# First key and query halves in banks of their own, longer transfer times in the planned order, and the last output tiles in score tile and free banks

## The chip, the cores and the metric

The kernel runs on one core of a Trainium2 chip. The metric is device time in microseconds (us) of one execution; three executions of the kernel before the change were timed. A profile of one more execution gives a span (from the first to the last instruction) and a record of every instruction and transfer. Engines are named as the profile names them: PE (TensorE matmuls), DVE (VectorE), ACT (ScalarE), POOL (GpSimd) and SP, the queue from which nearly all transfers (DMAs) are issued.

## The reference

A layer normalisation of x feeds two branches, whose outputs are added to x: causal attention with a memory that is carried over four segments of 512 tokens (32 heads of width 16), and a two-layer block with silu.

```python
x = A_x                                   # (1, 2048, 512), bf16
xn = _layernorm(x, axis=-1)
return x + _A_ref(xn, A_wq, A_wk, A_wv, A_wo, A_beta) + _B_ref(xn, B_w1, B_w2)

# _A_ref, for each segment s of 4, with q, k, v = xn @ wq, xn @ wk, xn @ wv by heads:
p = _softmax(qs @ ks.T * scale + mask)    # causal
a_dot = p @ vs
a_mem = (phi(qs) @ M) / (phi(qs) @ z + 1e-06)
o = g * a_mem + (1.0 - g) * a_dot         # g = sigmoid(beta)
M = M + phi(ks).T @ vs;  z = z + phi(ks).sum()
# after the segments: o @ wo

# _B_ref: silu(xn @ w1) @ w2, w1 (512, 1792), w2 (1792, 512)
```

## The kernel before

The program is written as a list of tasks. Each task has an engine, a duration `dur`, a time `vis` after which its result counts as visible to others, a due time, the tasks it depends on, and the buffers that it takes from a ring and gives back. `Sched.run` plays these tasks through with the durations and `vis` numbers written in the code, picks at each free engine the ready task with the earliest due time (with some rules of its own for scores, exponentials and evictions), and emits the instructions in the order in which they started in that play. That order is what each engine's instruction stream gets; an engine takes its stream in order, and an instruction whose input isn't there holds everything behind it on its engine. So a `vis` number that is too short puts a reader of a transfer too early in its engine's stream. `T0` and `CYC` set the due times (`Dn(n)`).

The on-chip accumulator memory is held as `psS`, one tile of four banks for the attention scores, and a ring `banks` of four single-bank tiles `ps66` to `ps69` for everything else. A write of PE into a bank tile waits until earlier reads of that tile are done, and a reader waits for the earlier writes.

The work of a segment s:

- `ln(s)`: statistics and normalised x (`xn`), transposed into `xnT` (segment 0 by PE and a copy, the others by transposing DMAs on SP).
- `k_tile`, `q_tile`, `v_tile`: `xnT` by `w_k`, `w_q`, `w_v`. Index u = 4 s + dt counts tiles of 128 of the 512 columns. `kB` is the key tile masked for even and odd heads, `kT` and `qT` the plain copies. The tile u = 0 goes through `first_tile`, in four pieces of 128 tokens, so that the first score can start early. `v_swap` makes `VS`, a copy of `V` with its partition halves swapped, by two DMAs.
- `quad(u, q)`: score n (`S{n}`) into `psS`, one exponential over 128x2048 on ACT (`E{n}`, tile `Pt`), and the causal mask on POOL (line 826). There are 72 of these. `pv` multiplies `Pt` by `V` and `VS`; DVE copies the results to `N` and `O`.
- `norm(s, dts)`: the softmax denominators of `N` and `O` go to DRAM (`dZ`), come back as `Zg`, are inverted by DVE (`Zf`, line 1028) and scaled by POOL (`Zr`), go to DRAM again (`dR`) and come back spread over all partitions as `R`; meanwhile `O` is merged into `N` by four DMAs. DVE multiplies `N` by `R` (line 1055). `den(s)` does the same for the memory's denominators (`dD`, `Dg`, `Dq`, `dE`, `Dr`), POOL multiplies `pq` by `Dr` (line 991), PE multiplies `pq` by the memory `Mbf`, and DVE adds that to `N` (line 1070). In the last segment `norm` runs for the first three column tiles, and then for the fourth alone.
- `h_tile`: xn by w1, tanh on ACT, gate on DVE (`hT`, line 1089). `w2_rows` and `wo_rows` give the output rows of segments 0 to 2.
- `tail()`: the last segment's four output tiles. Output tile j is 14 matmuls by `w_2` and 4 by `w_o`, all into `psS[:, j, :]`, then one eviction with the addition of x (`o_t`, line 1178) and a store.

Of the kernel before, what the change touches and what calls it, by code (L numbers as in the profile page):

```python
# [14 lines left out]
P = 128  # L15
# [6 lines left out]
NSEG = 4  # L22
# [19 lines left out]
NWARM = 44  # L42
# [4 lines left out]
PVW = 0.0  # L47

# [212 lines left out]
def kernel(  # L261
# [158 lines left out]
    load_x(12, 4, "SP", 0.7, 19.5)  # L420
# [117 lines left out]
    def ln(s, due):  # L538
        for half in range(2):
            ag = []  # L540
            for j in (2 * half, 2 * half + 1):
                t = s * TPS + j
                b = Buf(st_r)

                def f_st(t=t, b=b):
                    nc.vector.bn_stats(out=b.tile[:], in_=xt(t))
                    nc.vector.bn_aggr(out=mv[:, t, :], in_=b.tile[:])

                ag.append(A("DVE", 0.75, f_st, [xl[t]], due, takes=(b,), frees=(b,), label="stats"))
# [9 lines left out]
            for j in (2 * half, 2 * half + 1):  # L559
# [36 lines left out]
                else:  # L596
# [5 lines left out]
                    e = A("SP", 1.25, f_d, [n], due, vis=2.7, takes=(xnT_b[s],),  # L602
# [34 lines left out]
    def first_tile(w, loads, due, label):  # L637
        b = Buf(banks)
        pcs = []
        for j in range(TPS):  # L640
            c = slice(j * P, (j + 1) * P)

            def f(c=c):
                for ki in range(DT):
                    mm(b.tile[:, c], w[:, ki, 0:P], xnT_b[0].tile[:, ki, c], ki == 0, ki == DT - 1)
            pcs.append(A("PE", 0.26, f, [xnT_done[0][j], loads], due + 0.01 * j, takes=(b,),
                         frees=(b, xnT_b[0]), mode="full", label=label))
        return b, pcs
# [4 lines left out]
    def k_tile(s, dt, due):  # L653
        u = 4 * s + dt
        kT[u], kB[u] = Buf(kT_r), Buf(kB_r)
        if u == 0:
            b, pcs = first_tile(w_k, ld_k[0], due, "k0")
            kb_ev[u] = []
            for hf in range(2):
                c = slice(256 * hf, 256 * hf + 256)  # L660
                for r in range(2):
                    def f_e(c=c, r=r, hf=hf):
                        o = half(kB[u].tile, r, hf)
                        i = b.tile[:, c].rearrange("p (a b) -> p a b", b=KB)
                        if r == 0:
                            nc.scalar.mul(o, i, pm[:, 0:1])
                        else:
                            nc.vector.tensor_scalar(
                                out=o, in0=i, scalar1=pm[:, 1:2], scalar2=None, op0=ALU.mult
                            )  # L670
                    kb_ev[u].append(A(
                        "DVE" if r else "ACT", 0.3, f_e, pcs[2 * hf : 2 * hf + 2] + [c_pm], due + 0.5,
                        takes=(kB[u],), frees=(b, kB[u]), label="k0"))
            ev = A("DVE", 0.6, lambda: nc.vector.tensor_copy(out=kT[u].tile[:], in_=b.tile[:]),
                   pcs, due + 3, takes=(kT[u],), frees=(b, kT[u]), label="kT")
        else:
# [5 lines left out]
            ev = A("DVE", 0.6, lambda: nc.vector.tensor_copy(out=kT[u].tile[:], in_=b.tile[:]),  # L682
                   [g], due + 1.5, takes=(kT[u],), frees=(b, kT[u]), label="kT")
            kb_ev[u] = []
            for r in range(2):
                def f_o(r=r):
                    nc.gpsimd.tensor_scalar(  # L687
                        out=kB[u].tile[:, :, KB * r : KB * r + KB],
                        in0=kT[u].tile[:].rearrange("p (a b) -> p a b", b=KB),
                        scalar1=pm[:, r : r + 1], scalar2=1.0, op0=ALU.mult, op1=ALU.mult,  # L690
                    )
                kb_ev[u].append(pool(0.75, f_o, [ev, c_pm], due + 3, takes=(kB[u],),
                                     frees=(kT[u], kB[u]), label="kB"))
        if s < NSEG - 1:
            pb = Buf(pkT_r)
            zc = zc_t[s % 2][:, dt : dt + 1]
            f = phi(kT[u], pb, [ev], Dn(5 * u + 7), zc)
# [6 lines left out]
            e = A("SP", 1.25, f_t, [f], Dn(5 * u + 9), vis=2.7,  # L704
# [3 lines left out]
    def q_tile(s, dt, due):  # L708
        u = 4 * s + dt
        qT[u] = Buf(qT_r)  # L710
        if u == 0:
            b, pcs = first_tile(w_q, ld_q[0], due, "q0")
            q_ev[u] = []
            for hf in range(2):
                c = slice(256 * hf, 256 * hf + 256)

                def f_e(c=c, hf=hf):
                    if hf:
                        nc.scalar.copy(out=qT[u].tile[:, c], in_=b.tile[:, c])
                    else:  # L720
                        nc.vector.tensor_copy(out=qT[u].tile[:, c], in_=b.tile[:, c])
                q_ev[u].append(A("ACT" if hf else "DVE", 0.3, f_e, pcs[2 * hf : 2 * hf + 2],
                                 due + 0.5, takes=(qT[u],), frees=(b, qT[u]), label="q0"))
# [30 lines left out]
    def v_swap(s, due):  # L754
        ts = []
        for r in range(2):
# [3 lines left out]
            ts.append(A("SP", 0.5, f, v_ev[s], due, vis=3.5, takes=(VS_b[s],),  # L760
# [26 lines left out]
    def quad(u, q):  # L787
# [16 lines left out]
        deps = [d for uu in us for d in kb_ev[uu] + q_ev[uu]]  # L804
# [127 lines left out]
    def den(s, due):  # L932
# [25 lines left out]
        d1 = A("SP", 0.58, f_1, [e], due + 2, vis=2.7, frees=(db,), label="den")  # L958
# [3 lines left out]
        d2 = A("SP", 0.4, f_2, [d1], due + 3, vis=2.0, label="den")  # L962
# [14 lines left out]
        d3 = A("SP", 0.35, f_5, [r2], due + 6, vis=1.6, label="den")  # L977
        for dt in range(DT):
# [9 lines left out]
            d4 = A("SP", 0.45, f_6, [d3], due + 7, vis=3.6, takes=(rb,), frees=(rb,), label="den")  # L988
# [9 lines left out]
    def norm(s, dts, due, due_rep):  # L998
# [6 lines left out]
        for par in range(2):  # L1005
# [7 lines left out]
            zs.append(A("SP", 0.55, f_1, ev, due, vis=2.0, frees=(N_b[s] if par == 0 else O_b[s],),  # L1013
# [4 lines left out]
        d2 = A("SP", 0.45, f_2, zs, due + 1, vis=1.95, label="Z")  # L1018
        mg = []
        for g in range(4):  # L1020
# [3 lines left out]
            mg.append(A("SP", 0.6, f_m, [zs[0]] + [O_ev[4 * s + d] for d in dts] + [E_ev[4 * s + d] for d in dts], due + 1.5, vis=2.6,  # L1024
# [16 lines left out]
        d3 = A("SP", 0.35, f_5, [r2], due + 1, vis=1.6, label="Z")  # L1041
        for dt in dts:
# [8 lines left out]
            d4 = A("SP", 0.45, f_6, [d3], due + 1, vis=3.6, takes=(rb,), frees=(rb,), label="Z")  # L1051
# [96 lines left out]
    def tail():  # L1148
        s = NSEG - 1
        for j in range(TPS):  # L1150
            b = Fixed(psS[:, j, :])
            t = s * TPS + j

            def s2(ft, b=b, j=j):
                def f():
                    mm(b.tile[:], h_b[(s, ft)].tile[:, j * P : (j + 1) * P], w_2[:, ft, :],
                       ft == 0, False)
                return (f, 0.216, (h_ev[(s, ft)],))

# [14 lines left out]
            o.frees.append(N_b[s])  # L1174
            ob = Buf(o_r)

            def f_e(b=b, ob=ob, t=t):
                nc.vector.scalar_tensor_tensor(  # L1178
                    out=ob.tile[:], in0=b.tile[:], scalar=0.5, in1=xt(t), op0=ALU.mult,
                    op1=ALU.add,  # L1180
                )
            e = A("DVE", 0.6, f_e, [o], -2, takes=(ob,), frees=(ob,), label="o_t")
# [6 lines left out]
    for s in range(NSEG):  # L1189
# [3 lines left out]
        if s == 0:  # L1193
            for dt in range(DT):
                k_tile(0, dt, -2.9 if dt == 0 else Dn(5 * dt - 3 - dt % 2))
                q_tile(0, dt, -3 if dt == 0 else Dn(5 * dt - 2.9 - dt % 2))
                if dt == 0:
                    for j in range(TPS):
                        v_tile(0, j, Dn(0.2 + 0.7 * j))
                    v_swap(0, Dn(2))  # L1200
# [63 lines left out]
```

## Time and profile before

| what | value |
|---|---|
| three timed executions | 254.0, 255.46, 252.55 us; median 254.0 |
| profiled execution | own time 251.29 us, span 249.6 us |
| PE busy | 225.4 us, 90% of the span |
| DVE, ACT, POOL busy | 170.4, 178.4, 165.3 us |
| mean granted PE clock | 0.992 |
| transfers | 21.33 MB, 85 GB/s on average, up to 359 GB/s in the first 25 us |

The busy share of an engine is an average over stages. Where an engine stands idle, the profile names in square brackets what ended the wait and how long it was. The profiled execution's own time is 1.7 us longer than its span.

### The profile page before, as it was taken

The page shows a single profiled execution, that of the slowest core. Times are in us where ns is not written, and L with a number is a line of the kernel's source. Part 1 is how long each engine was busy: PE and PEld are TensorE (multiplying, and loading weights), DVE is VectorE, ACT ScalarE, POOL GpSimd, SP SyncE. Part 2 cuts the span into 40 slices and gives each one's busy share as a digit, 9 for nine tenths or more (in the row PEclk, how much of TensorE's full clock was granted, in tenths as well). Part 3 has the DMA queues.
Part 4 walks back from the last instruction along what each step waited for, and adds up shares of the span by engine and source line. Part 5 has one row for each costly group of instructions (what it writes and reads, how often), then busy time and mean ns, then how long its engine had stood idle before and what let it go on. Part 6 is the DMA issues. An engine that isn't in the chain of part 4 may idle for free.

```text
span 249.6 us, 6833 instructions
## 1 busy us (share of the span) xinstructions
PE 225.4 (90%) x2824; PEld 105.1 (42%) x2824; DVE 170.4 (68%) x298; ACT 178.4 (72%) x160; POOL 165.3 (66%) x279
## 2 busy tenths in 40 slices
PE   7889989989799869999898999999899999995973
PEld 7644344435343424443443444444353434441331
DVE  3569989977767647799824897766574866666132
ACT  2378978999788668978986898889968877720000
POOL 6328998789899488958865799479777455740000
PEclk9999999999999999999999999999999999999799
DMA  6999920014344242010364500133402000341001
GB/s 195 354 359 295 153 46 3 0 43 66 66 98 94 89 110 104 22 45 1 66 137 76 123 5 8 42 106 84 99 23 72 4 11 22 104 153 33 25 21 63
DMA packets 31068, 21.33 MB, mean 85 GB/s; under 512 B 16116, under 2 KB 30140, under 8 KB 31036
## 3 DMA queue, kind: packets, MB, share of 16 engines
q1 hardware_dynamic: 29692, 20.10, 31.4%
q10 hardware_dynamic: 1344, 0.79, 1.0%
q8 instruction: 22, 0.36, 0.6%
q14 instruction: 10, 0.08, 0.1%
HBM read 11.87 MB, written 2.65 MB: 58 GB/s over the span
## 4 chain that ended last, share of the span: by engine, by line
PE 40%; ACT 13%; DVE 13%; DMA 13%; POOL 10%; SPq 5%; issue 4%; ACTq 0%; DVEq 0%; POOLq 0%
PE ps L496 30%; ACT Pt L810 10%; PE psS L496 10%; POOL Pt L826 5%; DMA R<-dR 3%; DVE hT L1089 2%; DMA VS<-V 2%; DVE pkT L628 2%; DVE pq L628 2%; ACT hT L1085 2%; DMA dR<-Zr 2%; POOL kB L687 2%; DMA dZ<-O 1%; SPq L1047 1%; SPq L1023 1%
## 5 line engine op out<-in xcount | busy, mean ns | idle before, releaser
L810 ACT ACTIVATE Pt<-psS 128x2048 bf16<-128x2048 f32 x72 | 135.4, 1880 | 26.9 <-PE psS L496 24.0
L826 POOL TENSOR_SCALAR_AFFINE_SELECT Pt<-Pt 64x512 bf16<-64x512 bf16 (+1 forms) x144 | 94.3, 655 | 29.0 <-ACT Pt L810 23.9
L496 PE MATMUL ps<-xnT,w 128*128 128x512 bf16 x224 | 57.6, 380 | 0.0
L1089 DVE SCALAR_TENSOR_TENSOR hT<-hT,ps 128x512 bf16<-128x512 bf16 x56 | 37.2, 679 | 11.2 <-ACT hT L1085 11.2
L496 PE MATMUL ps<-w,hT 128*128 128x512 bf16 x168 | 41.9, 380 | 1.1 <-DVE acc L1114 1.1
L1085 ACT ACTIVATE hT<-ps 128x512 bf16<-128x512 f32 x56 | 32.1, 599 | 5.0 <-PE ps L496 5.0
L496 PEld LDWEIGHTS <-hT 128*128 128x128 bf16 x224 | 20.6, 99 | 31.3 <-issue 9.9
L496 PE MATMUL psS<-qT,kB 32*128 32x256 bf16 (+5 forms) x640 | 28.7, 261 | 2.9 <-ACT Pt L810 2.5
L496 PEld LDWEIGHTS <-w 128*128 128x128 bf16 x224 | 20.2, 98 | 24.5 <-issue 2.7
L687 POOL TENSOR_SCALAR kB<-kT,pm 128x512 bf16<-128x512 bf16 x30 | 21.6, 727 | 7.2 <-DVE kT L682 5.9
L496 PEld LDWEIGHTS <-kB 32*128 32x128 bf16 x640 | 12.5, 92 | 28.3 <-issue 27.1
L496 PE MATMUL ps<-Pt,VS 64*32 64x256 bf16 (+5 forms) x640 | 18.9, 261 | 3.4 <-DMA VS<-V 1.4
L496 PE MATMUL ps<-Pt,V 64*32 64x256 bf16 (+5 forms) x640 | 20.6, 260 | 0.2 <-DVE hT L1089 0.2
L496 PE MATMUL ps<-xnT,w_k 128*128 128x512 bf16 (+1 forms) x76 | 17.7, 346 | 2.6 <-DVE M L901 1.3
L496 PE MATMUL psS<-w,hT 128*128 128x512 bf16 x56 | 15.5, 401 | 3.1 <-DVE o_t L1178 2.3
L496 PE MATMUL ps<-xnT,w_q 128*128 128x512 bf16 (+1 forms) x76 | 17.2, 346 | 1.1 <-DVE hT L1089 0.8
L496 PE MATMUL ps<-w_v,xnT 128*128 128x512 bf16 x64 | 17.2, 380 | 0.0
L496 PEld LDWEIGHTS <-V 64*32 64x32 bf16 x640 | 13.7, 91 | 8.1 <-issue 3.2
L1055 DVE TENSOR_TENSOR N<-N,R 128x512 bf16<-128x512 bf16 x16 | 8.1, 510 | 12.0 <-DMA R<-dR 12.0
L869 DVE CAST N<-ps 128x512 bf16<-128x512 f32 x16 | 11.0, 687 | 7.7 <-PE ps L496 7.5
L496 PE MATMUL ps<-w_o,N 128*128 128x512 bf16 x48 | 12.9, 380 | 2.4 <-DVE N L1055 2.3
L496 PEld LDWEIGHTS <-VS 64*32 64x32 bf16 x640 | 12.7, 91 | 5.2 <-issue 1.8
(81 smaller groups left out, 261.8 us busy)
## 6 DMA issues: line engine op xcount, KB each, us to landing
VS<-V SPq DMA_DIRECT2D x8, 264.0 KB
R<-dR SPq DMA_DIRECT2D x16, 128.0 KB
out_dram<-o_t SPq DMA_DIRECT2D x16, 128.0 KB
w<-in_B_w_dram SPq DMA_DIRECT2D x2, 896.0 KB
w<-in_B_w_dram SPq DMA_DIRECT2D x1, 1792.0 KB
Dr<-dE SPq DMA_DIRECT2D x12, 128.0 KB
x_all<-in_A_x_dram SPq DMA_DIRECT2D x2, 512.0 KB
N<-O SPq DMA_DIRECT2D x12, 64.0 KB
```

The lines of the kernel that those rows point to most:

```text
L496: nc.tensor.matmul(o, lhsT=l, rhs=r, start=start, stop=stop, **k)
L628: nc.vector.scalar_tensor_tensor(out=dst_b.tile[:], in0=src_b.tile[:], scalar=0.0, in1=dst_b.tile[:], op0=ALU.max, op1=ALU.add, accum_out=acc,
L687: nc.gpsimd.tensor_scalar(out=kB[u].tile[:, :, KB * r : KB * r + KB], in0=kT[u].tile[:].rearrange("p (a b) -> p a b", b=KB), scalar1=pm[:, ...
L810: nc.scalar.activation(out=pb.tile[:], in_=psS[:], func=AF.Exp, scale=SCALE)
L826: nc.gpsimd.affine_select(out=v, in_=v, compare_op=ALU.is_ge, fill=0.0, base=0, pattern=pat, channel_multiplier=-1,)
L869: nc.vector.tensor_copy(out=dst.tile[:, dt, :], in_=buf.tile[:])
L1023: nc.sync.dma_start(out=N_b[s].tile[r, ds, :], in_=O_b[s].tile[r, ds, :])
L1047: nc.sync.dma_start(out=rb.tile[:], in_=dap(dR[i], (dt - dts[0]) * L, [[nd * L, 8], [0, DH], [1, L]]),)
L1055: nc.vector.tensor_tensor(out=v, in0=v, in1=rb.tile[:], op=ALU.mult)
L1085: nc.scalar.activation(out=hb.tile[:], in_=b.tile[:], func=AF.Tanh, scale=0.5)
L1089: nc.vector.scalar_tensor_tensor(out=hb.tile[:], in0=hb.tile[:], scalar=1.0, in1=b.tile[:], op0=ALU.add, op1=ALU.mult)
```

## The change

1. `first_tile` makes two of the four pieces of tile u = 0 per call, and `k_tile` and `q_tile` call it once for each half, so each half of the first key and query tile takes a bank tile of its own. `kT` of that tile is copied in two halves. Score 0 depends on the first half's `kB` pieces alone (and on both halves of `qT`). Six of the 44 pairs of filler matmuls (`NWARM`) go.
2. The `vis` numbers of nearly all transfers get longer: `dZ` 2.0 to 3.2 (2.5 for the last `norm`), `Zg` 1.95 to 2.6 (2.5), `R` 3.6 to 4.0 (3.2), `dD` 2.7 to 3.0, `Dg` 2.0 to 2.4, `Dr` 3.6 to 4.2, `xnT` 2.7 to 3.6, `VS` 3.5 to 6.0 in segment 0 and 4.2 in the others; the due times of V and `VS` in segment 0 move earlier. Since the order comes from these numbers, nearly every engine's stream changes in places.
3. In `tail()` output tiles 0 and 1 stay in `psS`, tiles 2 and 3 take bank tiles of the ring. The evictions of tiles 0 and 1 wait for both tiles; all evictions are written after all matmuls.

```diff
-NWARM = 44
+NWARM = 38
+ZW = (3.2, 2.5)
+ZG = (2.6, 2.5)
+ZD = (2.0, 1.6)
+ZR = (4.0, 3.2)
...
-    def first_tile(w, loads, due, label):
+    def first_tile(w, loads, due, label, hf):
         b = Buf(banks)
         pcs = []
-        for j in range(TPS):
-            c = slice(j * P, (j + 1) * P)
+        for j in (2 * hf, 2 * hf + 1):
+            c, o = slice(j * P, (j + 1) * P), slice((j % 2) * P, (j % 2) * P + P)
...
-            b, pcs = first_tile(w_k, ld_k[0], due, "k0")
-            kb_ev[u] = []
+            kb_ev[u], ev = [], []
             for hf in range(2):
-                c = slice(256 * hf, 256 * hf + 256)
+                b, pcs = first_tile(w_k, ld_k[0], due + 0.3 * hf, "k0", hf)
...
+                def f_c(hf=hf, b=b):
+                    nc.vector.tensor_copy(
+                        out=kT[u].tile[:, 256 * hf : 256 * hf + 256], in_=b.tile[:, 0:256]
+                    )
...
-            ts.append(A("SP", 0.5, f, v_ev[s], due, vis=3.5, takes=(VS_b[s],),
+            ts.append(A("SP", 0.6, f, v_ev[s], due, vis=6.0 if s == 0 else 4.2, takes=(VS_b[s],),
...
-        deps = [d for uu in us for d in kb_ev[uu] + q_ev[uu]]
+        deps = [d for uu in us for d in (kb_ev[uu][0:2] if n == 0 else kb_ev[uu]) + q_ev[uu]]
...
-        d2 = A("SP", 0.45, f_2, zs, due + 1, vis=1.95, label="Z")
+        d2 = A("SP", 0.55, f_2, zs, due + 1, vis=ZG[i == NSEG], label="Z")
...
-            b = Fixed(psS[:, j, :])
+            b = Fixed(psS[:, j, :]) if j < 2 else Buf(banks)
...
-            e = A("DVE", 0.6, f_e, [o], -2, takes=(ob,), frees=(ob,), label="o_t")
+            e = A("DVE", 0.6, f_e, [o] if j >= 2 else [ends[0][1], ends[1][1]], -2,
+                  takes=(ob,), frees=(ob,) + ((b,) if j >= 2 else ()), label="o_t")
...
-                        v_tile(0, j, Dn(0.2 + 0.7 * j))
-                    v_swap(0, Dn(2))
+                        v_tile(0, j, Dn(0.2 * j - 1))
+                    v_swap(0, Dn(-5))
```

Three places show how the streams move. The first is ACT at the program's start, from the copies that make `xnT` to the first exponential, `Pt_107<-psS`. Before:

```order
L590 COPY xnT_77<-ps_66 128x4x128
L590 COPY xnT_77<-ps_67 128x4x128
L590 COPY xnT_77<-ps_68 128x4x128
L719 CAST qT_90<-ps_66 128x256
L666 ACTIVATE kB_85<-ps_67,pm 128x4x64 x2
L619 ACTIVATE pkT_98<-kT_82 128x512
L810 ACTIVATE Pt_107<-psS 128x2048
```

and of the change:

```order
L594 COPY xnT_77<-ps_66 128x4x128
L594 COPY xnT_77<-ps_67 128x4x128
L594 COPY xnT_77<-ps_66 128x4x128
L669 ACTIVATE kB_85<-ps_69,pm 128x4x64
L727 CAST qT_90<-ps_68 128x256
L669 ACTIVATE kB_85<-ps_66,pm 128x4x64
L818 ACTIVATE Pt_107<-psS 128x2048
L623 ACTIVATE pkT_98<-kT_82 128x512
```

The two halves of `kB` now come from two banks, and the exponential of the memory's key tile (`pkT`) moves behind the first attention exponential.

The second is SP in the first segment's `norm` and the second segment's `den`, where `R` has three buffers, so that the fourth `R` (the second `R_139`) waits for the first to be used. Before:

```order
L1040 DMA dR_192<-Zr_176 128x128
L961 DMA Dg_179<-dD_198 128x128
L1047 DMA R_139<-dR_192 128x1x512
L1047 DMA R_140<-dR_192 128x1x512
L1047 DMA R_141<-dR_192 128x1x512
L976 DMA dE_202<-Dq_181 128x128
L984 DMA Dr_142<-dE_202 128x1x512
L984 DMA Dr_143<-dE_202 128x1x512
L1047 DMA R_139<-dR_192 128x1x512
```

and of the change:

```order
L1048 DMA dR_192<-Zr_176 128x128
L709 DMA_TRANSPOSE phiK_100<-pkT_99 128x4x128
L1055 DMA R_139<-dR_192 128x1x512
L1055 DMA R_140<-dR_192 128x1x512
L1055 DMA R_141<-dR_192 128x1x512
L969 DMA Dg_179<-dD_198 128x128
L1055 DMA R_139<-dR_192 128x1x512
L984 DMA dE_202<-Dq_181 128x128
```

The fourth `R` now stands ahead of `dE` and of both `Dr`, and `Dg` behind the first three `R`.

The third is SP in the last segment, from the first `norm`'s way back (`dR_195`) to the last `norm`'s read (`Zg_172`). Before:

```order
L1040 DMA dR_195<-Zr_177 96x128
L1145 DMA out_dram<-o_t_150 128x512
L1047 DMA R_139<-dR_195 128x1x512
L1047 DMA R_140<-dR_195 128x1x512
L1047 DMA R_141<-dR_195 128x1x512
L1145 DMA out_dram<-o_t_151 128x512
L1008 DMA dZ_191<-N_137 4x512
L1008 DMA dZ_191<-O_138 4x512
L1023 DMA N_137<-O_138 16x512
L1017 DMA Zg_172<-dZ_191 32x128
```

and of the change:

```order
L1048 DMA dR_195<-Zr_177 96x128
L1153 DMA out_dram<-o_t_150 128x512
L1055 DMA R_139<-dR_195 128x1x512
L1016 DMA dZ_191<-N_137 4x512
L1016 DMA dZ_191<-O_138 4x512
L1055 DMA R_140<-dR_195 128x1x512
L1055 DMA R_141<-dR_195 128x1x512
L1153 DMA out_dram<-o_t_151 128x512
L1031 DMA N_137<-O_138 16x512
L1025 DMA Zg_172<-dZ_191 32x128
```

The two `dZ` writes pass two `R` reads and a store. On POOL at the same time, the last causal mask, `Pt_108`, moved ahead of the multiplications of `pq` by `Dr`. Before:

```order
L826 AFFINE_SELECT Pt_107<-Pt_107 64x8x64 x2
L991 TENSOR_TENSOR pq_103<-pq_103,Dr_144 128x512
L1033 TENSOR_SCALAR Zr_177<-Zf_175,gcol 96x128
L991 TENSOR_TENSOR pq_104<-pq_104,Dr_142 128x512
L826 AFFINE_SELECT Pt_108<-Pt_108 64x8x64 x2
```

and of the change:

```order
L834 AFFINE_SELECT Pt_107<-Pt_107 64x8x64 x2
L834 AFFINE_SELECT Pt_108<-Pt_108 64x8x64 x2
L1041 TENSOR_SCALAR Zr_177<-Zf_175,gcol 96x128
L999 TENSOR_TENSOR pq_103<-pq_103,Dr_144 128x512
L999 TENSOR_TENSOR pq_104<-pq_104,Dr_142 128x512
```

PE's last product of `Pt` by `V` waits for that mask.

89 lines of the change are left out of this document (50 added, 39 removed).

## Prediction

> **What bounds the kernel now.** I read the busy shares first, then the chain of waits by engine, then busy time in stretches.
>
> ```profile
> PE 225.4 (90%) x2824; PEld 105.1 (42%) x2824; DVE 170.4 (68%) x298; ACT 178.4 (72%) x160; POOL 165.3 (66%) x279
> ...
> PE 40%; ACT 13%; DVE 13%; DMA 13%; POOL 10%; SPq 5%; issue 4%; ACTq 0%; DVEq 0%; POOLq 0%
> ...
> 32.00:80.00 48.00, 45.71 (x634) 20.77 (x635) 39.26 (x73) 41.93 (x42) 42.19 (x65) 1.00 0.25 49
> ...
> 130.00:214.00 84.00, 80.77 (x1119) 35.94 (x1116) 57.09 (x91) 70.87 (x60) 58.64 (x89) 1.00 0.20 53
> ...
> 231.00:250.00 19.00, 12.70 (x48) 4.98 (x48) 4.02 (x7) 0.00 (x0) 0.06 (x1) 0.88 0.10 35
> ```
>
> In the stretches (length, then PE, weight loads, DVE, ACT, POOL) PE is busy 45.7 of 48 us and 80.8 of 84 us. So the middle is bound by PE, and the other engines matter where they let PE wait. The change takes no real matmul away, so it can win only PE's waits. In the last 19 us PE is busy for 12.7, with ACT and POOL done: that stage is bound by a chain of waits, at a mean granted clock of 0.88.
>
> **The start.** These rows come from the timeline; the bracket is the idle time before the instruction and what ended it.
>
> ```profile
> 8.34 0.84 POOL L448 TENSOR_SCALAR_AFFINE_SELECT bmask<-bmask 128x128 bf16<-128x128 bf16 x2
> 8.62 0.75 PE L577 MATMUL ps<-ident,xn 128*128 128x128 bf16 x8 [0.16 <-DVE xn L564]
> 9.05 0.59 ACT L590 COPY xnT<-ps 128x512 bf16<-128x512 bf16 x1 [0.25 <-PE ps L577]
> ...
> 10.40 0.62 PE L496 MATMUL ps<-xnT,w_q 128*128 128x128 bf16 x8 [0.37 <-DVE qT L721]
> ...
> 11.58 0.48 DVE L668 TENSOR_SCALAR kB<-ps,pm 128x256 bf16<-128x256 f32 x1 [1.24 <-PE ps L496]
> ...
> 12.12 0.38 PE L496 MATMUL ps<-xnT,w_k 128*128 128x128 bf16 x4 [0.65 <-DVE kB L668]
> ...
> 12.59 0.84 ACT L666 ACTIVATE kB<-ps,pm 128x256 bf16<-128x256 f32 x2 [1.16 <-PE ps L496]
> ...
> 13.55 0.39 PE L496 MATMUL psS<-qT,kB 32*128 32x512 bf16 x4
> 13.86 0.68 DVE L674 CAST kT<-ps 128x512 bf16<-128x512 f32 x1
> ...
> 14.58 0.63 ACT L619 ACTIVATE pkT<-kT 128x512 bf16<-128x512 bf16 x1 [1.15 <-DVE kT L674]
> ...
> 15.12 1.86 ACT L810 ACTIVATE Pt<-psS 128x2048 bf16<-128x2048 f32 x1
> ```
>
> Before, the halves share a bank: PE waits 0.37 us until DVE has read the first query half and 0.65 us until it has read the first key half, and only then can ACT make `kB`. Score 0 starts at 13.55; ACT takes `pkT` before the first exponential, which starts at 15.12.
>
> Now step by step for the change. POOL puts `bmask` (8.06 to 9.12 with its memset, about 1.0 us) ahead of the second reciprocal root, so the third and fourth normalised tiles come some 0.45 us later. PE has placed three pieces ahead of their transposes as well, so these start at about 9.4 instead of 8.62. ACT's copy starts 0.43 us into them and takes 0.59, DVE's copy is there at about 10.65. Then come four pieces, at 0.24 us each from about 10.55 (eight matmuls take 0.62 with the last one's tail), to 11.5. ACT's first `kB` half (0.42, half of 0.84) needs only the first two pieces and DVE's (0.48) ends at about 11.5. Score 0 follows at **11.7, 1.85 us earlier**, and the first exponential at about 12.2, 2.9 us earlier, since `pkT` is now behind it. The six pairs of filler matmuls stood in the wait that is gone; they are worth nothing more. `kT` in halves costs DVE about 0.2 us (two 256-wide reads at the 0.48 above, one of which stands in a wait).
>
> Unknown: score 0 now stands behind a first `V` matmul, which needs `w_v`. Before, that matmul came after score 0 and did not wait, so the weight was there by 13.87. If it lands as late as that, score 0 is 0.5 us late instead (minus 0.5 to plus 1.85). SP's timeline narrows that:
>
> ```profile
> 10.84 1.23 SPq L389 DMA_DIRECT2D w<-in_B_w_dram  x1
> ```
>
> This load of `w_2` waits for the same semaphore as `w_v`, and its issue ended at 12.07. I take 1.85.
>
> **The first `VS`.** The chain of waits and the timeline:
>
> ```profile
> 12.11 5.71 SPq L378 DMA_DIRECT2D x_all<-in_A_x_dram  x1
> ...
> 26.60 5.53 DMA VS<-V
> ...
> 32.17 0.40 PE L496 MATMUL ps<-Pt,VS 64*32 64x512 bf16 x8 [1.42 <-DMA VS<-V]
> ```
>
> PE lost 1.42 us to it. In the change all `V` matmuls come before the second key tile: 16 at 0.22 us and two scores after 11.7 give `V` at about 17.5, just when SP is through with its loads (12.11 + 5.71 = 17.82). `VS` goes out there, 7 us earlier. Queued behind the weights it may take longer than 5.53, but it has until about 28.5. The wait goes. Start and `VS` together: 1.85 + 1.42 = 3.3, from 0.9 (late `w_v`) to 3.3; I take **3.0**, with DVE's extra 0.2.
>
> **The middle.** From the list of waits, SP's timeline and DVE's:
>
> ```profile
> PE ps L496 <- DVE N L1055: 2.3, 1, 2.3
> ...
> PE ps L496 <- DVE acc L1114: 2.0, 2, 1.1
> ```
>
> ```profile
> 82.31 2.51 SPq L1047 DMA_DIRECT2D R<-dR  x3
> ...
> 88.94 0.57 SPq L1047 DMA_DIRECT2D R<-dR  x1
> ...
> 92.72 0.56 DVE L1055 TENSOR_TENSOR N<-N,R 128x512 bf16<-128x512 bf16 x1 [2.91 <-DMA R<-dR]
> ...
> 132.32 0.95 DVE L1028 RECIPROCAL Zf<-Zg 128x128 f32<-128x128 bf16 x1 [4.57 <-DMA Zg<-dZ]
> ```
>
> Those 4.3 us of PE are transfers that came later than planned: DVE stood at the head of its stream before a product or a reciprocal, and the evictions behind it held PE's banks. The fourth `R` was issued at 88.94, behind `dE` and two `Dr`; in the change only the first `R`'s use is ahead of it, so it can go out some 2.5 us earlier, and the 2.3 us wait should go. The longer `dZ` and `Zg` numbers move the other reciprocals back in DVE's stream. Against that, every stream is new, and new waits will come. Bounds: plus 4.3, and minus 3 if as many new ones of this size (about 1 to 2 us) appear; I take **1.5**.
>
> **The end.** Timeline of ACT, POOL, DVE, SP and PE, and one row of the list of waits:
>
> ```profile
> 214.39 1.90 ACT L810 ACTIVATE Pt<-psS 128x2048 bf16<-128x2048 f32 x1
> ...
> 217.91 1.38 POOL L826 TENSOR_SCALAR_AFFINE_SELECT Pt<-Pt 64x512 bf16<-64x512 bf16 x2
> ...
> 221.30 0.68 DVE L869 CAST O<-ps 128x512 bf16<-128x512 f32 x1
> ...
> 221.22 1.86 SPq L1047 DMA_DIRECT2D R<-dR  x3
> ...
> 223.68 0.53 SPq L1008 DMA_DIRECT2D dZ<-N  x1
> ...
> 227.02 0.53 SPq L1017 DMA_DIRECT2D Zg<-dZ  x1
> ...
> 229.65 0.94 DVE L1028 RECIPROCAL Zf<-Zg 32x128 f32<-32x128 bf16 x1 [2.41 <-DMA Zg<-dZ]
> ...
> 235.49 0.43 DVE L1055 TENSOR_TENSOR N<-N,R 128x512 bf16<-128x512 bf16 x1 [4.36 <-DMA R<-dR]
> ...
> 231.19 0.39 PE L496 MATMUL psS<-w_o,N 128*128 128x512 bf16 x1 [2.06 <-DVE N L1070]
> 231.42 2.08 PE L496 MATMUL psS<-w,hT 128*128 128x512 bf16 x5
> ...
> 234.57 3.45 PE L496 MATMUL psS<-w,hT 128*128 128x512 bf16 x14
> ...
> 246.28 0.69 DVE L1178 SCALAR_TENSOR_TENSOR o_t<-psS,x_all 128x512 bf16<-128x512 f32 x1 [1.98 <-PE psS L496]
> ...
> PE psS L496 <- DVE o_t L1178: 2.3, 3, 0.8
> ```
>
> Four losses. The last mask starts at 217.91, 1.6 us after its exponential (216.29), behind two `pq` products. `dZ` goes out 1.7 us after `O` is there (221.98), behind three `R` and a store. PE waits 2.06 us at the reciprocal, and the next five matmuls go at 0.42 us instead of 0.216. And since all four tiles lie in `psS`, PE waits 0.78 us three times for an eviction of another tile.
>
> In the change, on the same clock: the mask runs at 216.4, the last product of `Pt` at 217.9, `O` is there at 220.5. SP's first `R` still waits for `dR` to about 221; `dZ` follows at 221.6 (2.1 earlier), so `Zg` lands at about 227.6. After the reciprocal (0.87), one product (0.34) and the addition (0.62), PE gets its next `N` tile at 229.5. PE has 45 matmuls in its stream between the last product of `Pt` (1.15 long) and that point: 219.05 + 45 x 0.216 = 228.8, so it waits 0.7 us, not 2.06. Behind that stand 44 matmuls, 9.5 us: 239.0 against 246.25. The last `R` comes 6.3 us after `Zg` (235.92 - 229.65 before), one `Dr` later: 234.5, just when PE reaches its partner product (22 matmuls, 234.3). The two tiles in `psS` are ready 13 matmuls before PE's end, so their joint eviction costs nothing. That is 7.2 us; PE's smaller waits for gates and evictions aren't in it, so I take **6.0**. Bounds: 3.0 if only the eviction waits and part of the first stall go, and 7.2.
>
> On the slow matmuls: between 231.42 and 234.57 PE made eight matmuls (five by `hT`, three by `N`) at about 0.4 us, after a 2.06 us gap; at 0.216 us they take 1.7 instead of 3.15. That is 1.4 us, and the sum has it gone. [...]
>
> **Sum.** 3.0 + 1.5 + 6.0 = 10.5 us. From the profiled execution's own 251.29 that gives 240.8; the timed runs' median is 254.0, 2.7 above that execution, so I predict **243.5** for the median.
>
> **Rivals.**
> - *Only the end gains.* The early lead is eaten: DVE, ACT or POOL hold the scores back to their old times. For it: all are over 90% busy from 20 to 30 us (columns as above).
>
> ```profile
> 20.00:30.00 10.00, 10.00 (x68) 3.97 (x64) 9.90 (x20) 9.48 (x9) 9.23 (x17) 1.00 1.07 217
> ```
>
> Against it: ACT and POOL start their chains 2.9 us earlier too. Gain 4 to 7: 247 to 250.
> - *New waits at reciprocals make it slower.* Seven transfers end at a reciprocal at the head of DVE's stream before the last one. At the end one of them cost PE 2.06 us and the slow clock 1.4, 3.5 together. If the seven each cost that, 24.5 us instead of the 2.0 now charged to `acc`, it is 22.5 - 10.5 = 12 us slower, 266; it decides from 13 us, 1.9 us on each. For it: the places in DVE's stream are all new. Against it: the transfer numbers went up, and the 4.57 us wait of DVE above cost PE under 1.2 us.
> - *The order hardly changes what waits* (new waits equal old ones, the end gains 2 or 3 by the evictions and loses as much by its own): 252 to 255.
> - *Everything comes.* 3.3 + 4.3 + 7.2 = 14.8: 239.
>
> **Chances.** My forecast (240.5 to 246.5) 0.57, only the end 0.22, everything 0.08, hardly a change 0.08, slower 0.05. Range 239.5 to 250.5: it leaves out the last two and the edges of the second and third. A measurement of this kernel tells about 1% (2.5 us) from no change. Faster by more 0.87, within 0.08, slower 0.05.
>
> **What would show it.** Score 0 near 11.7 and the first exponential near 12.2 (else `w_v` was late); no PE wait on `VS`; no PE wait over 2 us on `N` from line 1055's product; `dZ` of the last column right behind `O`; one PE stall under 1 us near the last reciprocal, full clock behind it, and no PE wait on the last evictions. I would be wrong if PE's waits between 32 and 214 us grew, with DVE idle ahead of a reciprocal or a product with `R`.

## Result and the profile after

Four executions of the changed kernel took 243.62, 241.7, 247.51 and 243.12 us, median 243.4; four of the kernel before beside them took 253.3 in the median. The ratio is 0.958, interval 0.947 to 0.969. (Ratios here compare executions within 1.5% of each kernel's fastest.) The profiled execution took 243.62 us, with a span of 241.9, against 251.29 and 249.6 before: 7.7 us less.

First the page of the changed kernel (busy shares, granted clock by fortieths of the span, chain of waits by engine), then two stretches with the columns as in the prediction (the last three are granted clock, DMA share and GB/s), then PE's list of waits (total, times, longest):

```profile
PE 223.8 (93%) x2812; PEld 104.8 (43%) x2812; DVE 170.2 (70%) x299; ACT 178.5 (74%) x160; POOL 164.0 (68%) x279
...
PEclk9999968999999997999999999999999999999999
...
PE 39%; POOL 16%; DMA 15%; DVE 12%; ACT 10%; SPq 4%; issue 3%; POOLq 0%; ACTq 0%; DVEq 0%
```

```profile
32.00:80.00 48.00, 45.59 (x594) 20.45 (x580) 39.10 (x71) 41.76 (x40) 39.12 (x59) 0.93 0.21 45
80.00:130.00 50.00, 46.95 (x640) 21.36 (x639) 36.35 (x64) 39.63 (x34) 37.33 (x58) 0.97 0.29 77
```

The second of these stretches in the kernel before:

```profile
80.00:130.00 50.00, 44.81 (x634) 20.66 (x633) 35.69 (x62) 40.58 (x34) 37.28 (x56) 1.00 0.29 75
```

```profile
PE ps L500 <- DVE hT L1097: 6.9, 5, 3.6
...
PE psS L500 <- DVE N L1078: 1.3, 1, 1.3
```

The waits for `o_t`, for `acc` and for `N` behind `R` are off the list. In their place PE waits 6.9 us for gates (`hT`), and the clock is 0.93 and 0.97 in stretches where it was 1.00. The busy time of PE hides that: 45.59 of 48 us is as much as before, but part of it is at half the clock.

**The start, and where its gain went.** Timelines of PE, ACT, SP and DVE, and one row of the chain (the DMA row):

```profile
11.17 0.40 PE L500 MATMUL psS<-qT,kB 32*128 32x512 bf16 x4
11.62 1.88 ACT L818 ACTIVATE Pt<-psS 128x2048 bf16<-128x2048 f32 x1
...
17.79 1.98 SPq L767 DMA_DIRECT2D VS<-V  x2
20.13 9.98 SPq L602 DMA_TRANSPOSE xnT<-xn  x4
20.13 8.25 DMA xnT<-xn
28.47 0.41 DVE L568 TENSOR_SCALAR xn<-x_all,mv,rstd 128x512 bf16<-128x512 bf16 x1 [3.48 <-DMA xnT<-xn]
30.39 0.66 DVE L1097 SCALAR_TENSOR_TENSOR hT<-hT,ps 128x512 bf16<-128x512 bf16 x1
31.10 0.40 PE L500 MATMUL ps<-Pt,VS 64*32 64x512 bf16 x8 [3.64 <-DVE hT L1097]
```

Score 0 starts at 11.17 (13.55 before), the first exponential at 11.62 (15.12). `VS` goes out at 17.79, some 8 us earlier than before. But then DVE's fourth normalisation for segment 1 stands at the head of its stream. `xn` has three buffers, and the transposing DMA that reads the wanted one, issued at 20.13, is through after 8.25 us. Behind it in DVE's stream, 1.9 us of work later, stands the gate (30.39) whose bank PE needs. So the first product of `Pt` by `VS` (the first product, below; the first PV in the expectations) starts at 31.10 where it was 32.17: of 3.5 us, 1.07 are left. The granted clock then is at half from 31.5 to 38.4 us, which costs at most 3.4 us by my estimate (half of 6.8), and the lead is gone.

**The end.** Timelines of POOL, DVE, SP and PE:

```profile
214.97 1.38 POOL L834 TENSOR_SCALAR_AFFINE_SELECT Pt<-Pt 64x512 bf16<-64x512 bf16 x2 [1.38 <-ACT Pt L818]
218.26 0.68 DVE L877 CAST O<-ps 128x512 bf16<-128x512 f32 x1
220.09 0.55 SPq L1016 DMA_DIRECT2D dZ<-N  x1
225.81 0.94 DVE L1036 RECIPROCAL Zf<-Zg 32x128 f32<-32x128 bf16 x1 [0.79 <-DMA Zg<-dZ]
233.66 0.43 DVE L1063 TENSOR_TENSOR N<-N,R 128x512 bf16<-128x512 bf16 x1 [5.44 <-DMA R<-dR]
234.94 0.60 PE L500 MATMUL psS<-w_o,N 128*128 128x512 bf16 x2 [1.26 <-DVE N L1078]
235.58 1.29 DVE L1197 SCALAR_TENSOR_TENSOR o_t<-psS,x_all 128x512 bf16<-128x512 f32 x2 [0.70 <-PE psS L500]
```

The mask runs right behind its exponential, `dZ` goes out 1.2 us after `O` is there, PE has no stall at the reciprocal, no half clock and no wait for an eviction; it waits once, 1.26 us, for the product with the last `R`. That `R` came later than worked out: its product ends 8.3 us after the start of the last reciprocal (6.3 before); `dR`, issued at 228.43, stood behind three merges and a `Dr`, which is part of it.

The lead at an exponential is its start before minus its start in another kernel's profile (us), from ACT's timelines, one profile of each kernel; "to the end" is the span minus the start of the last exponential (before: 214.39, and 35.2 to the end):

| exponential | after | new tail alone | all but the tail | 4 xn buffers | same, old tail | same, old Z times |
|---|---|---|---|---|---|---|
| 6 | 3.6 | 0.1 | 2.8 | 3.1 | 3.2 | 3.2 |
| 9 | -0.5 | 0.0 | -3.1 | 3.1 | 3.1 | 0.6 |
| 24 | 0.6 | 0.6 | -2.9 | 3.4 | 3.4 | 1.7 |
| 27 | 4.3 | 0.4 | 0.8 | 7.2 | 7.2 | 5.0 |
| 30 | 1.0 | 0.4 | -1.1 | 6.4 | 6.6 | -1.6 |
| 42 | 1.6 | 0.4 | -1.4 | 8.5 | 8.2 | -0.3 |
| 71 | 1.4 | -1.0 | -2.2 | 9.2 | 8.9 | -0.3 |
| to the end | 28.9 | 31.2 | 33.2 | 30.1 | 29.7 | 30.6 |

Up to the last exponential the changed kernel is only 1.36 us ahead; the other 6.3 of its 7.7 us are the end's. These leads differ between executions: a second profile of the changed kernel, further below, has -3.9 at exponential 9, -2.4 at the last and 29.6 to the end.

### The profile page after: what moved, and what is told of

It is laid out like the page before. It is cut to its first block, busy times and chain, and to the rows that moved or that the text cites. A ratio compares the mean times of both kernels' runs of the same rounds, so it can differ in the third digit from the quotient of the medians.

```text
span 241.9 us, 6809 instructions
## 1 busy us (share of the span) xinstructions
PE 223.8 (93%) x2812; PEld 104.8 (43%) x2812; DVE 170.2 (70%) x299; ACT 178.5 (74%) x160; POOL 164.0 (68%) x279
## 4 chain that ended last, share of the span: by engine, by line
PE 39%; POOL 16%; DMA 15%; DVE 12%; ACT 10%; SPq 4%; issue 3%; POOLq 0%; ACTq 0%; DVEq 0%
PE ps L500 32%; ACT Pt L818 8%; POOL Pt L834 8%; PE psS L500 6%; DMA xnT<-xn 3%; POOL kB L695 3%; DMA R<-dR 2%; DVE st L550 2%; SPq L1031 2%; DMA Dg<-dD 2%; POOL pq L999 2%; ACT hT L1093 2%; DMA dR<-Zr 2%; DVE hT L1097 2%; DMA Dr<-dE 1%
## 5 line engine op out<-in xcount | busy, mean ns | idle before, releaser
L818 ACT ACTIVATE Pt<-psS 128x2048 bf16<-128x2048 f32 x72 | 135.3, 1879 | 31.2 <-PE psS L500 26.5
L500 PE MATMUL ps<-xnT,w 128*128 128x512 bf16 x224 | 57.0, 383 | 0.1
L500 PE MATMUL ps<-w,hT 128*128 128x512 bf16 x196 | 48.7, 380 | 0.0
L500 PE MATMUL ps<-Pt,VS 64*32 64x256 bf16 (+5 forms) x640 | 20.1, 273 | 4.7 <-DVE hT L1097 4.5
L695 POOL TENSOR_SCALAR kB<-kT,pm 128x512 bf16<-128x512 bf16 x30 | 20.8, 702 | 4.2 <-DVE kT L690 2.7
L500 PE MATMUL ps<-Pt,V 64*32 64x256 bf16 (+5 forms) x640 | 21.8, 271 | 0.0
L500 PE MATMUL ps<-xnT,w_k 128*128 128x512 bf16 (+1 forms) x76 | 19.7, 366 | 0.5 <-DVE N L877 0.5
L999 POOL TENSOR_TENSOR pq<-pq,Dr 128x512 bf16<-128x512 bf16 x12 | 13.8, 1158 | 6.2 <-DMA Dr<-dE 5.9
L500 PE MATMUL ps<-w_o,N 128*128 128x512 bf16 x56 | 15.1, 384 | 1.2 <-DVE hT L1097 1.2
L500 PE MATMUL ps<-w_v,xnT 128*128 128x512 bf16 x64 | 16.0, 380 | 0.0
```

What stands on the lines that cost most here:

```text
L500: nc.tensor.matmul(o, lhsT=l, rhs=r, start=start, stop=stop, **k)
L695: nc.gpsimd.tensor_scalar(out=kB[u].tile[:, :, KB * r : KB * r + KB], in0=kT[u].tile[:].rearrange("p (a b) -> p a b", b=KB), scalar1=pm[:, ...
L818: nc.scalar.activation(out=pb.tile[:], in_=psS[:], func=AF.Exp, scale=SCALE)
L999: nc.gpsimd.tensor_tensor(out=pb.tile[:], in0=pb.tile[:], in1=rb.tile[:], op=ALU.mult)
```

## Experiments

### Where the early lead goes

The theory: the change's own early lead is lost to the full `xn` ring, as above. The rival: DVE, ACT and POOL, all over 90% busy there, would hold the scores back anyway. Four buffers first:

```diff
-    xn_r = ring(3, [P, D], BF16, "xn")
+    xn_r = ring(4, [P, D], BF16, "xn")
```

> The changed kernel with four buffers for normalised tiles in place of three; the order of each engine's instructions stays the same up to the first PV and past it. Theory A (the early lead of 3.3 us is lost because DVE's fourth normalisation stands at the head of its stream until a transposing DMA has read the third-last tile, 3.48 us, and the gate behind it holds PE for 3.64 us, with 6.8 us of half clock after it): no such wait on DVE, the first PV at about 27.5 instead of 31.1, full clock behind it. The lead of 3.7 us that went between scores 6 and 9 stays: 243.4 - 3.7 = 239.7; with as much of it lost in the middle as the lead table of the two profiles shows elsewhere, 241.5. Rival C (DVE, ACT or POOL, each over 90% busy there, hold the scores back anyway): PE waits at the same place for another engine, and the time stays at 243 to 244.

Measured: 238.0 us, ratio 0.945, 0.940 to 0.950. The timelines of DVE and PE at the same place:

```profile
25.04 1.20 DVE L568 TENSOR_SCALAR xn<-x_all,mv,rstd 128x512 bf16<-128x512 bf16 x2
28.48 0.66 DVE L1097 SCALAR_TENSOR_TENSOR hT<-hT,ps 128x512 bf16<-128x512 bf16 x1
29.19 0.40 PE L500 MATMUL ps<-Pt,VS 64*32 64x512 bf16 x8 [1.21 <-DVE hT L1097]
```

Both normalisations run on, no DVE wait for a buffer stands there, the clock stays full in this profile (1.00 from 20 to 40 us), and the lead of 3.1 us is kept past exponential 9. The rival falls. Against the changed kernel that is 5.4 us by the medians and 3.3 us by the two ratios to before, about the 3.7 expected.

As a control, the same line in the kernel before:

> The kernel before with four buffers for normalised tiles. Its DVE never waited for such a buffer near the first PV, whose orders stay as they were; the streams behind 40 us are planned anew. Theory A (the fourth buffer pays only because the change made DVE wait for one): 252.9, from 250.5 to 254. Rival D (the fourth buffer, or the new plan that comes with it, is worth some 5 us by itself): 248.

Measured: 253.8 us, ratio 1.002, 0.997 to 1.006. The fourth buffer is worth nothing without the change, and a new plan behind 40 us is no gain by itself.

Next the other way to the same place, the planner's number for segment 1:

```diff
-                    e = A("SP", 1.25, f_d, [n], due, vis=3.6, takes=(xnT_b[s],),
+                    e = A("SP", 1.25, f_d, [n], due, vis=8.0 if s == 1 else 3.6, takes=(xnT_b[s],),
```

> The changed kernel, with the planner told that the second segment's transposing DMAs take 8.0 us instead of 3.6 (8.25 us in the profile). The planner then puts the gate that PE waited for ahead of the fourth normalisation on DVE; the buffers stay three. Theory A: the first PV comes at about 28, without a half clock behind it, 239.5 to 242. Rival C: another engine takes the place, 243 to 244. Since every stream behind that place is new as well, a new wait of 2 us in the middle would make it look like C; the first PV in the profile tells them apart.

Measured: 241.1 us, ratio 0.956, 0.951 to 0.960, inside the range. Timeline of PE, and two stretches:

```profile
29.54 0.40 PE L500 MATMUL ps<-Pt,VS 64*32 64x512 bf16 x8 [1.84 <-DVE hT L1097]
```

```profile
32.00:34.00 2.00, 0.89 (x2) 0.41 (x3) 2.00 (x5) 2.00 (x2) 0.51 (x2) 0.50 0.61 129
34.00:36.00 2.00, 2.00 (x16) 0.58 (x15) 1.83 (x9) 0.18 (x2) 1.24 (x3) 0.50 0.07 14
```

The wait shrinks to 1.84 us, but the clock (third column from the right, 0.50) still halves here, which the expectation had not: by the time, the order alone gives part of what the buffer gives.

Then the cause of the late transfers, with one DMA moved:

```diff
-    ld_2 = load_w(w_2[:], kv(B_w2), "SP", 0.5, 18.0)
+    ld_2 = load_w(w_2[:], kv(B_w2), "SP", 0.5, 8.0)
...
                     v_swap(0, Dn(-5))
+                    for d in xnT_done[1]:
+                        d.outs.append((ld_2, False))
+                        ld_2.nwait += 1
```

> The changed kernel with one transfer moved: the load of w_2 (1792 KB), which is issued at 10.6 us, goes out behind the fourth transposing DMA instead; no other instruction on any engine changes its place, and the normalised tiles keep three buffers. Theory A1 (the transfers of V and the transposing DMAs are late because they queue behind the weights): VS lands about 5.5 us after its issue as in the kernel before, or sooner, DVE's 3.48 us wait ahead of the fourth normalisation goes, the first PV comes at about 27.5 with full clock behind it: 243.4 - 3.7 = 239.7. Theory A2 (the transposing DMAs are slow by themselves, one behind the other and behind VS): DVE still waits some 3 us there, 243.

Measured: 246.4 us, where the changed kernel took 246.3 beside it; ratio to before 0.972, 0.965 to 0.980. Neither theory had this. Timelines and, for `phiK`, the chain:

```profile
16.33 1.18 SPq L767 DMA_DIRECT2D VS<-V  x2
24.62 1.18 DVE L568 TENSOR_SCALAR xn<-x_all,mv,rstd 128x512 bf16<-128x512 bf16 x2
28.37 0.40 PE L500 MATMUL ps<-Pt,VS 64*32 64x512 bf16 x8 [0.73 <-DVE hT L1097]
27.72 0.58 SPq L393 DMA_DIRECT2D w<-in_B_w_dram  x1
28.40 7.95 DMA phiK<-pkT
36.44 0.63 ACT L623 ACTIVATE pkT<-kT 128x512 bf16<-128x512 bf16 x1 [4.36 <-DMA phiK<-pkT]
38.88 0.62 PE L500 MATMUL psS<-qT,kB 32*128 32x512 bf16 x4 [3.82 <-ACT Pt L818]
```

A1 (late behind the load) was right on the spot: without the load ahead of them the transposing DMAs are in time, DVE does not wait, and the first product comes at 28.37. But the load (1792 KB) now stands ahead of the transposing DMA of `phiK`, which takes 7.95 us (4.82 in the profile with four `xn` buffers, where the load went out at 12.19); `pkT` has two buffers, ACT waits 4.36 us at its head, and PE 3.82 us behind it. The wait moved to another queue. With four buffers:

> Four buffers for normalised tiles, and the load of w_2 behind the transposing DMAs; against the kernel with four buffers only that load moves. With four buffers VS lands about when the first PV needs it, and PE waits 1.2 us there for a gate. If the weights delay VS (A1), VS comes earlier and the first PV is at about 27 us: 238.0 - 1.0 = 237.0. Under A2 it stays 238.0.

Measured: 239.8 us, ratio 0.949, 0.942 to 0.957. The same wait appears, 4.83 us on ACT and 4.10 on PE, and no earlier product (29.09). So a third buffer for `pkT`:

```diff
-    pkT_r = ring(2, [P, L], BF16, "pkT")
+    pkT_r = ring(3, [P, L], BF16, "pkT")
```

> Four buffers for normalised tiles, the load of w_2 behind the transposing DMAs of the second segment, and three buffers in place of two for the feature maps of the keys (pkT), whose transposing DMAs stand behind that load. With two, ACT stood 4.4 us at the head of its stream until such a DMA had read its buffer, and PE waited 4.1 us for the exponential behind it. If that wait is the same mechanism at another engine, the third buffer ends it: 239.8 - 3.8 = 236.0, from 235.5 to 237.5. If the load of w_2 costs as much elsewhere: 239 to 240.

Measured: 238.0 us, ratio 0.957, 0.950 to 0.963. ACT's wait for `phiK` is off its list of waits, as expected, and the lead at exponential 9 is 3.5 us; the time missed its range by 0.5 us. The order behind that place is planned anew, and the lead at the last exponential is 7.6 us, where two profiles of four `xn` buffers alone had 9.2 and 7.2; what the 0.5 us are is not shown. It equals that kernel within the spread.

The changed kernel and the kernel with four `xn` buffers were run again:

> The changed kernel once more, beside the next three on one chip: 243.4. The wait ahead of the first PV was 3.64 us in the first profile and 6.7 us in the kernel with the old last tiles, whose order up to there is the same. If that wait varies from execution to execution, the times of this kernel spread over some 4 to 6 us, more than those of the kernel with four buffers (2.0 us over four runs).

Measured: 243.8 to 248.1 us over four executions, a spread of 4.3, median 246.3, ratio 0.966, 0.956 to 0.976. Its profile is of the 248.1 us execution:

```profile
32.57 0.41 DVE L568 TENSOR_SCALAR xn<-x_all,mv,rstd 128x512 bf16<-128x512 bf16 x1 [5.59 <-DMA xnT<-xn]
35.20 0.62 PE L500 MATMUL ps<-Pt,VS 64*32 64x512 bf16 x8 [6.07 <-DVE hT L1097]
```

The median missed 243.4 by 2.9 us, and the spread was as expected. PE's wait is 3.64, 6.07 and 6.67 us in three profiles with the same order up to there (the third is of the kernel with the old last tiles). In the two with the longer wait the transposing DMAs were issued at 22.49 and 21.65 us instead of 20.13 and took 9.99 and 10.58 us instead of 8.25. So this wait varies with the arrival of the transfers; that it makes the whole spread is not shown.

> The kernel with four buffers for normalised tiles once more, beside the next three on one chip: 238.0, from 237 to 239.

Measured: 239.1 us, 235.3 to 240.4, ratio 0.953, 0.940 to 0.966. That is just above its range. This version and the one with the third `pkT` buffer are the best of those with the change whole, 238 to 239 us. The profile of this second measurement has slow matmuls that the first had not, right behind a wait of 1.50 us for the gate: twelve score matmuls of 32x256 take 0.61 us from 32.91, and twelve of the same shape 0.40 from 35.59. The lead at exponential 9 is 1.0 us there. So the fourth buffer ends DVE's wait for the ring, but PE goes at full pace behind the first product in one profile of two. The claim of a narrower spread holds for its first four executions (2.0 us) and not for these six (5.1).

### What the end is worth, and by what

The new last tiles alone, on the kernel before:

```diff
-            b = Fixed(psS[:, j, :])
+            b = Fixed(psS[:, j, :]) if j < 2 else Buf(banks)
...
-            e = A("DVE", 0.6, f_e, [o], -2, takes=(ob,), frees=(ob,), label="o_t")
+            e = A("DVE", 0.6, f_e, [o] if j >= 2 else [ends[0][1], ends[1][1]], -2,
+                  takes=(ob,), frees=(ob,) + ((b,) if j >= 2 else ()), label="o_t")
```

> The kernel before with the last four output tiles alone changed: two in the score tile, two in free banks, the evictions after the last matmuls. Order and numbers elsewhere stay as before. Theory A (banks and order both made the end's 6.3 us): the three waits of PE for an eviction (2.3 us) go, the stall of 2.06 us at the last reciprocal and the slow matmuls behind it stay. 253.3 - 2.3 = 251.0, from 250 to 251.5. Rival B (the split tiles made it all): 253.3 - 6.3 = 247.0, and the stall at the last reciprocal shrinks too, since the two tiles in free banks give PE other work there.

Measured: 249.3 us, ratio 0.985, 0.980 to 0.990: 3.9 us, between the two (in this profile a half clock from 135.6 to 139.0 us took 1.5 us of lead besides). Timeline of PE:

```profile
232.65 0.39 PE L496 MATMUL psS<-w_o,N 128*128 128x512 bf16 x1 [2.30 <-DVE N L1070]
232.88 1.24 PE L496 MATMUL psS<-w,hT 128*128 128x512 bf16 x5
```

The stall at the last reciprocal stays (2.30 us), so B falls; but the matmuls behind it go at full clock (five in 1.24 us, 2.08 before), which A had not counted on. From the last exponential to the end it takes 31.2 us instead of 35.2. Some 1.4 of these 4.0 us are the clock, and the tiles did not shorten the stall: the clock was at half behind 2.06 us before and is at 1.00 behind 2.30 us here, and what decided is not shown. The rest is near A's 2.3.

The opposite edit, the old last tiles in the changed kernel:

> The changed kernel with the last four output tiles as before, all in the score tile. Theory A: PE's waits for evictions come back, 2.3 us, and the rest of the end's gain (the mask right behind its exponential, the transfer of Z straight behind O) stays: 243.4 + 2.3 = 245.7, from 245 to 246.7. Rival B: the whole 6.3 us of the end comes back: 249.7.

Measured: 250.3 us, ratio 0.989, 0.981 to 0.998. Near B's number, but for another reason: in this profile the wait ahead of the first product was 6.67 us (3.64 in the changed kernel's first), and the last exponential is 3.5 us later. The end itself takes 33.2 us against 28.9, 4.3 more. Timeline of PE, and a stretch:

```profile
239.24 0.59 PE L500 MATMUL psS<-w,hT 128*128 128x512 bf16 x2 [0.78 <-DVE o_t L1186]
240.62 1.44 PE L500 MATMUL psS<-w,hT 128*128 128x512 bf16 x3 [0.78 <-DVE o_t L1186]
242.84 1.87 PE L500 MATMUL psS<-w,hT 128*128 128x512 bf16 x4 [0.78 <-DVE o_t L1186]
```

```profile
241.00:242.00 1.00, 1.00 (x3) 0.30 (x2) 0.00 (x0) 0.00 (x0) 0.00 (x0) 0.50 0.38 131
```

The three eviction waits cost 2.3 us, and here the half clock came with them (0.50 from 241 us on), some 2 more by difference. So from 35.2 us the tiles take off 4.0 alone and 4.3 on top of the order, of which 2.3 are the eviction waits and most of the rest is the clock; the order (mask, `dZ`) takes off 2.0 alone. Mask and `dZ` were not tried one by one.

I then expected the tiles to be worth the same in the best version:

> Four buffers for normalised tiles, and the last four output tiles as in the kernel before, all in the score tile; the order of the transfers stays. From the last exponential to the end the profiles gave 35.2 us before, 31.2 with the new last tiles alone, 33.2 with the new order alone, 28.9 with both, so the banks are worth 4.0 to 4.3 us whatever the order: 238.0 + 4.1 = 242.1. If only PE's waits for an eviction counted (2.3 us), 240.3.

Measured: 237.1 us, ratio 0.949, 0.936 to 0.961, beside 239.1 with the new tiles: no loss at all, both numbers missed. Timeline of PE and DVE at its end:

```profile
227.89 1.46 PE L500 MATMUL psS<-w_o,N 128*128 128x512 bf16 x6
229.38 0.69 DVE L1186 SCALAR_TENSOR_TENSOR o_t<-psS,x_all 128x512 bf16<-128x512 f32 x1 [1.04 <-PE psS L500]
230.13 0.38 PE L500 MATMUL psS<-w_o,N 128*128 128x512 bf16 x1 [0.78 <-DVE o_t L1186]
```

Where PE came earlier to the end, all matmuls by `hT` are done before the last `N`, only one is left behind an eviction, and the chain from `dZ` over `R` sets the end: 29.7 us from the last exponential, 30.1 with the new tiles. Behind its last product by `V`, PE has 74 weight loads, one for each matmul, here and with the new tiles, 81 in the kernel before and 89 in the changed kernel. So the banks of their own took 4.0 us off the end on the kernel with 81 loads left and 4.3 on the one with 89, where PE still had a queue of other tiles' matmuls behind the evictions, and nothing on the one with 74.

### What the longer transfer numbers are worth in the middle

The old numbers for `dZ`, `Zg`, `dR`, `R`, `dD`, `Dg`, `dE`, `Dr` and the merge in the kernel with four buffers:

```diff
-ZW = (3.2, 2.5)
-ZG = (2.6, 2.5)
-ZD = (2.0, 1.6)
-ZR = (4.0, 3.2)
+ZW = (2.0, 2.0)
+ZG = (1.95, 1.95)
+ZD = (1.6, 1.6)
+ZR = (3.6, 3.6)
...
-        d1 = A("SP", 0.58, f_1, [e], due + 2, vis=3.0, frees=(db,), label="den")
+        d1 = A("SP", 0.58, f_1, [e], due + 2, vis=2.7, frees=(db,), label="den")
```

> Four buffers for normalised tiles, with the planner's old, shorter times for the transfers of the denominators, of Z and of R; the longer times of the transposing DMAs and of VS stay. If the longer numbers make the middle's gain of some 6 us (PE's waits for N behind a late R, and for acc behind a late Z), these come back: 238.0 + 4.3 = 242.3, with DVE waiting for R or Z ahead of a bank. If they change nothing that PE waits for: 238.0.

Measured: 244.9 us, ratio 0.975, 0.960 to 0.989, against 0.953 for the same kernel with the long numbers beside it. Timelines of SP, DVE and PE:

```profile
83.40 0.40 SPq L984 DMA_DIRECT2D dE<-Dq  x1
88.35 1.23 SPq L992 DMA_DIRECT2D Dr<-dE  x2
89.70 0.57 SPq L1055 DMA_DIRECT2D R<-dR  x1
93.41 0.51 DVE L1063 TENSOR_TENSOR N<-N,R 128x512 bf16<-128x512 bf16 x1 [3.62 <-DMA R<-dR]
93.97 0.61 PE L500 MATMUL ps<-w_o,N 128*128 128x512 bf16 x1 [3.93 <-DVE N L1063]
```

It is the wait of the kernel before (2.26 us there), larger: the fourth `R` behind `dE` and two `Dr`. Exponentials 27 to 30 lose 6.6 us of lead, with a half clock from 92.7 to 99.6 us. From exponential 9 to the last this kernel loses 0.9 us, and the two profiles with the long numbers gain 6.0 and 6.1. So the numbers of the transfers make the middle's gain there; how much of it holds in other executions is less sure, since this profile is of the slowest of four (247.1 us; the two fastest took 241.7 and 243.6, 2.6 and 4.5 above the long numbers). In it the clock also halved at the first product, before the edit has changed any order: 2.6 us of lead at exponential 9. PE's rows there, and behind them the one of the first profile with four buffers and long numbers that answers to the second, where the clock stayed full:

```profile
29.09 0.40 PE L500 MATMUL ps<-Pt,VS 64*32 64x512 bf16 x8 [1.14 <-DVE hT L1097]
32.01 0.59 PE L500 MATMUL ps<-xnT,w_k 128*128 128x512 bf16 x1 [1.40 <-DVE N L877]
```

```profile
32.14 1.44 PE L500 MATMUL ps<-xnT,w_k 128*128 128x512 bf16 x4 [1.44 <-DVE N L877]
```

## Why the prediction was right, step by step

The time, 243.4, is what was predicted (243.5); two of the three terms came out near their size, in the main for the reasons given, and the first did not.

- **The start, 3.0 predicted.** Score 0 and the first exponential came 0.5 us earlier than worked out, `w_v` was in time (the `V` matmul ahead of score 0 did not wait), and the lead was 3.6 us just ahead of the first product. PE's wait for `VS` at the head is gone. The step that failed is "The wait goes": behind it stood the next one. The working had `VS` queued behind the weights, but left out the transposing DMAs, which SP now issues behind `VS` and each of which holds an `xn` buffer. At the first product the term measured 1.07 instead of 3.0, near its lower bound of 0.9, which stood for another cause (a late `w_v`), and minus 0.5 with the half clock behind it. The prediction's rival "the early lead is eaten" is what happened, by a transfer and not by busy engines.
- **The middle, 1.5 predicted.** From exponential 9 to the last the lead grew by 1.9 us. The fourth `R` was issued at 85.72 (predicted some 2.5 us earlier than 88.94, measured 3.2), and no wait of PE for `N` behind `R` is left. The new waits are there as well: DVE stood 3.55 us at a reciprocal for `Dg`, PE waited 1.19 and 0.63 us for the gates behind it, and the clock was at half for 3.4 us:

```profile
89.25 0.95 DVE L973 RECIPROCAL Dg<-Dg 128x128 f32<-128x128 f32 x1 [3.55 <-DMA Dg<-dD]
91.48 0.81 PE L500 MATMUL ps<-w_o,N 128*128 128x512 bf16 x3 [1.19 <-DVE hT L1097]
93.25 0.61 PE L500 MATMUL ps<-Pt,VS 64*32 64x512 bf16 x8 [0.63 <-DVE hT L1097]
```

  With four `xn` buffers the middle gave 6.0 us (lead 3.1 to 9.2; 6.1 in the second profile), above the bound of 4.3: the two waits were there to be had, and some 1.7 us more that the list of waits did not show.
- **The end, 6.0 predicted, 6.3 measured.** `dZ` goes out 7.1 us after the last exponential's start instead of 9.3, 2.2 earlier (2.1 predicted); PE has no stall at the reciprocal; no eviction waits, no half clock. The stall, 0.7 us predicted, came at the last `R` instead, 1.26 us, where the working had `R` come 6.3 us after `Zg` and it took 8.3. The sum has the 1.4 us of slow matmuls gone, which was an estimate that the clock stays full behind a short stall: behind the 1.26 us it was at 1.00 (at half behind the 2.06 us before). What the prediction did not see is that the terms are not a sum of their own: by the experiments the tiles are 4.0 to 4.3 with the clock, the order 2.0, and in a kernel whose PE is earlier the tiles are worth nothing.
- **"I would be wrong if PE's waits between 32 and 214 us grew."** They did not (in sum PE was idle for 7.5 us there, 10.7 before); the loss stood just ahead of that stretch, and in the clock inside it.

So the total was right partly by luck: the start fell short by some 3.5 us against its 3.0, the middle and the end came out 0.7 above theirs, and the median lay 0.3 below the profiled execution, where 2.7 above it had been added. Beside the next experiments the same kernel measured 246.3.

## What to carry to other kernels

When a change lets one transfer go earlier, list what its queue issues behind it and which buffers those transfers hold: here the gain ended at the first ring that ran full (three `xn` buffers, a DVE wait of 3.48 us), and one more buffer there brought back 3.3 to 5.4 us. When a large load causes a wait, look at what stands behind its new place before moving it: with the 1792 KB load moved, DVE's wait of 3.48 us went and one of 4.36 came on ACT, at the next transfer issued behind the load. Before giving the last tiles banks of their own, count the work that PE still has queued behind the evictions: they took 4.0 and 4.3 us off the end with 81 and 89 matmuls left behind the last product by `V`, and nothing with 74.

## What was not expected of the hardware

- A transposing DMA issued behind a 1792 KB load took 7.95 us (`phiK`, the load moved), and one behind `VS` and the loads 8.25 us (`xnT`, changed kernel); that of `phiK` took 4.82 us with four `xn` buffers and the load in its old place.
- In the first profile of the changed kernel and in that of the kernel before, the clock was granted at half in these stretches up to its last matmul (for the last column, the 3.41 us ahead of each):

| profile | clock at half, us | for, us | PE busy ahead, us |
|---|---|---|---|
| changed kernel | 31.53 to 38.35 | 6.83 | 0.43 |
| kernel before | 231.68 to 235.09 | 3.41 | 1.35 |
| changed kernel | 92.97 to 96.38 | 3.41 | 1.88 |

  In the second profile of the changed kernel it was at half from about 30.7 to 41.0 us, and PE was busy for 0.98 of the 4 us from 28 to 32.
- Like waits did not end alike. In the kernel before, the clock halved behind a gap of 2.06 us; with the new tail alone it was at 1.00 behind one of 2.30. With four `xn` buffers PE was busy for 0.81 of the 2 us from 28 to 30, and the clock stayed at 1.00 to 42 us; with the old `Z` times it was busy for 0.91 of them, and the clock was at half from about 31.3 to 38.1. What decides is not shown; no run sets out to test it.
